# Five operations moved in the hand-written order of a local-attention and expert-adapter kernel

## Chip, cores and metric

The kernel runs on one core of a Trainium2 chip. The metric is the device time of one execution in microseconds, the median of the runs.

## What is computed

Causal attention over 8 batches x 8 heads x 576 tokens x 64 dimensions, in which heads 0 to 3 look back over 32 tokens and heads 4 to 7 over every fourth of 128 tokens; then, on the joined heads as rows of 512, a top-2 mixture of 8 rank-16 adapters that is added to its input. Cut to what matters:

```python
scores = q @ k.T / sqrt(64);  scores = where(mask, scores, -1e9)
x = softmax(scores) @ v                       # (4608, 512) after joining the heads
logits = x @ w_gate                           # (4608, 8)
topk = the two largest logits of a token;  w = softmax of these two
out = x + sum over e in topk of w[e] * ((x @ A[e]) @ B[e])
```

Softmax of two numbers is a sigmoid; the kernel makes it from a tanh of the logit's distance from the mean of the two.

## The kernel before

The work is cut into 8 rows, one for each batch; each row has two halves g = 0, 1 (plain heads, strided heads). `program()` builds named operations, each with an engine and the operations that it depends on. The text `PLAN` (line 605) lists all the names: `ordered()` and `run()` emit the instructions in just that order. An engine works through its own names one after the other, and an instruction whose input isn't there holds up everything behind it on its engine. A number behind @ is the PSUM bank at which a tile begins; a tile waits for all users of the tile that held the bank before it. Waits for other engines are semaphores; a wait that an earlier one already covers is left out.

The operations of a row r that matter here (r = 6 or 7 in the tail):

- `B`, `Bx`: the normalised attention output x is cast to bfloat16 (GpSimd, line 397; ScalarE, line 399). `T`, `U`: TensorE turns it (lines 414, 438). `C`, `Cx`, `Cd`, `Cp`: ScalarE (lines 424, 427, 430, 444, 448) and VectorE (line 431) copy it out of PSUM as xt.
- `Z0`, `Z1`: TensorE multiplies xt by the adapters' A and the gate weights (20 matmuls of 128x136, all TensorE products of this kind go through the helper on line 213). In rows 0 to 6 `Y0`, `Y1` copy the result to SBUF as zs (ScalarE, line 472); in row 7 it is read from PSUM.
- The gate on VectorE: `m0`, `m1` the two largest logits (lines 484, 485), `s12` their sum (line 486), `tt` twice the logit less the sum (line 489), `top` the comparison with the second largest (line 492), `g2` (named g26 for row 6: g2 of row 6) the gate (line 494). Between them stands `th`, the tanh on ScalarE (line 491).
- `gz`: the product of gate and low-rank result (line 499), on GpSimd in rows 0 to 6; in row 7 two pieces `gy`, `gz` on VectorE. `G` (in row 7 `G` and `H`): TensorE turns it (line 504). `gc`, `gn`, `gm`: copies of it out of PSUM, for the two halves (lines 518, 520, 523).
- `D0`, `D1`, `D3`: TensorE multiplies by the adapters' B, four or two matmuls of 128x256; `D2`: four of 64x128 for the last 64 tokens. `A0`, `A1`: VectorE adds the result to x (line 551). `dy`, `A3` and `dx`, `A2`: ScalarE copies a part of the result to SBUF (lines 557, 577), and GpSimd adds it (lines 559, 579).
- `O`: the store of x by SyncE's queue (lines 592, 601). Rows 0 to 4 are stored whole. `O51` waits for A51 and A52, `O50` for A50, A52 and A53, and likewise in row 6; row 7 is stored as `O71` (A71, A72; 576 KB), `O70` (A70; 256 KB) and `O70b` (A72, A73; 320 KB).

D51 is thus row 5's second product, A52 row 5's addition of the last tokens, and so on. The part of the list that makes the tail begins on line 631. What a name waits for is set where it is added, as in

```python
gz = add(f"{a}{r}", "POOL", ("el", 1230), lambda us=us: gates(us, nc.gpsimd), [g2, zc[0], zc[1]] + ([f"G{r - 2}"] if r > 1 else []))
gt.append(add(f"{b}{r}", "PE", ("t", len(us) * nk), lambda us=us, k=k: turn_g(us, k), [gz] + gt, k))
add(f"A{r}2", "POOL", ("el", 512), lambda: [nc.gpsimd.tensor_tensor(ends, ends, two(DY[0]), ALU.add)], [dx] + made)
```

Of the kernel before, what the change touches and what calls it, by code (L numbers as in the profile page):

```python
# [627 lines left out]
Lv701 B60 gz4 E170 E071 s125 G4@0 B61 D31@6 tt5 th5 gn4 V70@1 T60@4  # L628
A31 gc4 V71@5 U6@0 C60 O0 g25 O2 gz5 G5@4 Cp6 Cd6 R70 N70
B70 T61@2 D41@0 D42@3 R71 N71 gn5 A41 C61 dx4 gc5 B71 Bx7 D40@5  # L630
Z06@2 Y06 Z16@4 Y16 A40 m06 A42 D52@3 m16 s126 dx5 top6 U7@7 Cp7
Cd7 tt6 T71@1 Cx7 C71 T70@4 D51@5 A52 th6 g26 A51 D50@0 A50 C70
gz6 Z07@2 Z17 m07 m17 s127 tt7 dy5 G6@5 gc6 O3 O4 O51 D61@0 th7 gn6
D62@7 A53 top7 dx6 g27 D60@5 gy7 gz7 A62 dy6 O50 A61 A63
O61 G7@3 H7 gm7 gn7 gc7 D72@0 dx7 A72 D71@1 A60 D73@6 O60 A71
D70@7 O71 A70 O70 dy7 A73 O70b
"""

# [65 lines left out]
```

## Time and profile before

| what | value |
| --- | --- |
| median of 3 runs | 100.3 us (100.02 to 101.3) |
| the profiled execution's own time | 100.78 us |
| its span, first to last instruction | 99.0 us |
| instructions in the span | 3612 |
| mean granted TensorE clock over the span | 0.976 of full speed |

The span is what the trace covers; the execution's own time holds 1.8 us more around it. Engines are named PE (TensorE's matmuls; PEld are its weight loads), DVE (VectorE), ACT (ScalarE), POOL (GpSimd) and SP (SyncE); a q behind the name is the engine's queue. All times of rows are microseconds from the start of the span. The store O70b is issued at the end of A73, and the span ends once the last store has landed.

### The profile page before, as it was taken

The page shows a single profiled execution, that of the slowest core. Times are in us where ns is not written, and L with a number is a line of the kernel's source. Part 1 is how long each engine was busy: PE and PEld are TensorE (multiplying, and loading weights), DVE is VectorE, ACT ScalarE, POOL GpSimd, SP SyncE. Part 2 cuts the span into 40 slices and gives each one's busy share as a digit, 9 for nine tenths or more (in the row PEclk, how much of TensorE's full clock was granted, in tenths as well). Part 3 has the DMA queues.
Part 4 walks back from the last instruction along what each step waited for, and adds up shares of the span by engine and source line. Part 5 has one row for each costly group of instructions (what it writes and reads, how often), then busy time and mean ns, then how long its engine had stood idle before and what let it go on. Part 6 is the DMA issues. An engine that isn't in the chain of part 4 may idle for free.

```text
span 99.0 us, 3612 instructions
## 1 busy us (share of the span) xinstructions
PE 81.1 (82%) x1587; PEld 59.7 (60%) x1587; DVE 62.4 (63%) x138; ACT 71.4 (72%) x123; POOL 54.6 (55%) x73
## 2 busy tenths in 40 slices
PE   3999969878569989999897979999599988776500
PEld 2443556466446875789666868877487877564300
DVE  5770009506469189459735698779494999979810
ACT  5195692599848974896995689989389989957400
POOL 5999902862449044406941297098076463665820
PEclk9999999999999999999999999999999999999955
DMA  2999999999999999999999999999999996976894
GB/s 18 314 201 211 202 214 224 200 210 226 210 213 213 212 211 214 220 215 207 218 217 213 213 214 213 213 209 186 206 383 425 432 409 287 409 309 251 352 410 194
DMA packets 6095, 24.50 MB, mean 247 GB/s; under 512 B 832, under 2 KB 960, under 8 KB 5440
## 3 DMA queue, kind: packets, MB, share of 16 engines
q0 software_dynamic: 3920, 14.23, 72.1%
q1 hardware_dynamic: 2016, 9.77, 24.6%
q8 instruction: 12, 0.20, 0.8%
q10 hardware_dynamic: 144, 0.28, 0.7%
q14 instruction: 3, 0.02, 0.1%
HBM read 29.07 MB, written 9.44 MB: 389 GB/s over the span
## 4 chain that ended last, share of the span: by engine, by line
PE 45%; DMA 15%; ACT 15%; POOL 10%; DVE 6%; issue 5%; POOLq 0%
PE ps L213 37%; DMA in<-in_qkv_dram 15%; ACT p L351 8%; POOL in L273 7%; PE ps L414 5%; DVE x L390 3%; ACT xt L424 2%; PE ps L504 2%; ACT zs L472 2%; POOL x L559 1%; DVE x L551 1%; POOL xb L397 1%; ACT gn L523 1%; PE ps L438 1%; ACT th L491 1%
## 5 line engine op out<-in xcount | busy, mean ns | idle before, releaser
L397 POOL CAST xb<-x 128x1152 bf16<-128x1152 f32 (+1 forms) x16 | 18.3, 1143 | 25.6 <-DVE x L390 25.6
L351 ACT ACTIVATE p<-ps 128x960 bf16<-128x960 f32 (+1 forms) x32 | 27.6, 900 | 3.4 <-PE ps L213 3.2
L213 PE MATMUL ps<-in,p 128*64 128x130 bf16 (+1 forms) x416 | 21.5, 221 | 4.1 <-ACT p L351 2.9
L390 DVE TENSOR_TENSOR x<-ps,rec 128x1152 f32<-128x1152 f32 x16 | 21.7, 1357 | 0.5
L213 PEld LDWEIGHTS ps<-in,p 128*64 128x64 bf16 (+1 forms) x416 | 17.1, 104 | 7.5 <-ACT p L351 3.9
L551 DVE TENSOR_TENSOR x<-x,ps 128x1024 f32<-128x1024 f32 (+1 forms) x16 | 17.5, 1116 | 3.4 <-PE ps L213 3.4
L387 DVE RECIPROCAL rec<-ps 128x18 f32<-128x18 f32 x16 | 4.3, 270 | 17.7 <-PE ps L213 17.6
L499 POOL TENSOR_TENSOR gz<-zs,g 128x640 bf16<-128x640 f32 x7 | 8.9, 1275 | 9.4 <-DVE g L494 9.4
L213 PE MATMUL ps<-warm 128*128 128x512 f32 x22 | 12.4, 706 | 1.5 <-DVE warm L217 1.5
L213 PEld LDWEIGHTS ps<-in 64*64 64x64 bf16 x576 | 10.9, 106 | 2.7 <-issue 0.7
L213 PE MATMUL ps<-in 64*64 64x96 bf16 (+1 forms) x576 | 11.9, 201 | 0.5 <-issue 0.5
L273 POOL DMA_DIRECT2D in<-in_qkv_dram x22 | 11.8, 581 | 0.8 <-POOLq L687 0.8
L213 PE MATMUL ps<-aw,xt 128*128 128x136 bf16 x160 | 11.4, 223 | 0.4 <-issue 0.3
L424 ACT COPY xt<-ps 128x1024 bf16<-128x1024 bf16 x8 | 8.1, 1011 | 3.4 <-PE ps L414 3.3
L213 PEld LDWEIGHTS ps<-aw,xt 128*128 128x128 bf16 x160 | 9.6, 98 | 1.4 <-issue 0.4
L414 PE MATMUL ps<-one,xb 128*128 128x128 bf16 x128 | 9.6, 219 | 0.9 <-issue 0.8
L414 PEld LDWEIGHTS ps<-one,xb 128*128 128x128 bf16 x128 | 7.6, 98 | 2.2 <-issue 0.9
L427 ACT COPY xt<-ps 128x1024 bf16<-128x1024 bf16 x7 | 7.2, 1034 | 2.3 <-PE ps L414 2.3
L213 PEld LDWEIGHTS ps<-warm 128*128 128x128 f32 x22 | 4.6, 228 | 6.1 <-issue 4.6
L213 PE MATMUL ps<-bt,gn 128*128 128x256 bf16 (+1 forms) x48 | 6.8, 263 | 1.5 <-ACT gn L523 0.8
L213 PE MATMUL ps<-bt,gc 128*128 128x256 bf16 (+1 forms) x48 | 6.6, 255 | 1.5 <-ACT gc L520 1.5
L472 ACT COPY zs<-ps 128x408 f32<-128x408 f32 (+1 forms) x14 | 5.9, 451 | 2.0 <-PE ps L213 1.9
(55 smaller groups left out, 101.6 us busy)
## 6 DMA issues: line engine op xcount, KB each, us to landing
in<-in_qkv_dram POOLq DMA_DIRECT2D x5, 1152.0 KB, 23.2
out_dram<-x SPq DMA_DIRECT2D x5, 1152.0 KB, 7.6
in<-in_qkv_dram POOLq DMA_DIRECT2D x10, 292.5 KB, 24.0
in<-in_qkv_dram POOLq DMA_DIRECT2D x10, 288.0 KB, 8.2
out_dram<-x SPq DMA_DIRECT2D x5, 576.0 KB, 3.0
in<-in_qkv_dram POOLq DMA_DIRECT2D x10, 146.2 KB, 8.1
in<-in_qkv_dram POOLq DMA_DIRECT2D x2, 434.2 KB, 13.8
out_dram<-x SPq DMA_DIRECT2D x1, 320.0 KB, 3.4
```

Of the source, the lines that this page charges most:

```text
L213: return nc.tensor.matmul(o, lhsT=lhsT, rhs=rhs, start=start, stop=stop, skip_group_check=True)
L273: nc.gpsimd.dma_start(out=IN[r % SLOTS][half(a), at : at + n], in_=qkv[r, a, :, at - 2 * VB * a : at - 2 * VB * a + n],)
L351: return [nc.scalar.activation(p[:, :, :].rearrange("p h (s c) -> p h s c", c=PER)[:, :, b0 : b0 + nb, 0:SEG], PS[:, k.at : k.at + 2, 0 : ...
L387: rc = add(f"R{tag}", "DVE", ("el", 60), lambda: [nc.vector.reciprocal(rec[:, :].rearrange("p (b i) -> p b i", b=3), PS[:, k.at : k.at + 3 ...
L390: nm = add(f"N{tag}", "DVE", ("el", XG), lambda: [nc.vector.tensor_tensor(X[r][:, XG * g : XG * g + XG].rearrange("p (b i n) -> p b i n", ...
L397: add(f"B{tag}", "POOL", ("el", cut), lambda: [nc.gpsimd.tensor_copy(XB[r % 2][:, g, 0:cut], X[r][:, XG * g : XG * g + cut])], [nm] + free)
L414: nc.tensor.transpose(tp[j][:, 128 * u : 128 * u + 128], xb[:, g, 256 * u + 128 * j : 256 * u + 128 * j + 128], ident())
L424: return [nc.scalar.copy(xt[:, 0:2, 0:S].rearrange("p j (c i) -> p j c i", c=C)[:, :, :, 0:128], tp.rearrange("p j (i c) -> p j c i", c=C))]
L427: return [nc.scalar.copy(xt[:, 2:4, 0:512], tp)]
L472: zc.append(add(f"Y{st}{r}", "ACT", ("el", len(us) * ZW), lambda us=us, k=k: [nc.scalar.copy(zs[:, us[0] : us[-1] + 1].rearrange("p u n -> ...
L499: return [en.tensor_tensor(GZ[i][:, us[0] : us[0] + n, :].rearrange("p u (e r) -> p u e r", e=E), zv()[:, us[0] : us[0] + n, 0:ER].rearran ...
L551: return [nc.vector.tensor_tensor(v, v, PS[:, k.at : k.at + nk].rearrange("p b n -> p (b n)"), ALU.add)]
```

## The change

Five names move within the list. In row 6 tt6 goes ahead of top6 (VectorE), th6 ahead of C71 (ScalarE), A52 behind gz6 (GpSimd), and G6 ahead of Z07 and Z17 (TensorE). In row 7 D71 goes ahead of D72 (TensorE). The banks stay: G6 still takes bank 5, D71 bank 1, D72 bank 0. SyncE's order of stores is the same.

```diff
-Z06@2 Y06 Z16@4 Y16 A40 m06 A42 D52@3 m16 s126 dx5 top6 U7@7 Cp7
-Cd7 tt6 T71@1 Cx7 C71 T70@4 D51@5 A52 th6 g26 A51 D50@0 A50 C70
-gz6 Z07@2 Z17 m07 m17 s127 tt7 dy5 G6@5 gc6 O3 O4 O51 D61@0 th7 gn6
+Z06@2 Y06 Z16@4 Y16 A40 m06 A42 D52@3 m16 s126 dx5 tt6 top6 U7@7 Cp7
+Cd7 T71@1 Cx7 th6 C71 T70@4 D51@5 g26 A51 D50@0 A50 C70
+gz6 A52 G6@5 Z07@2 Z17 m07 m17 s127 tt7 dy5 gc6 O3 O4 O51 D61@0 th7 gn6
 D62@7 A53 top7 dx6 g27 D60@5 gy7 gz7 A62 dy6 O50 A61 A63
-O61 G7@3 H7 gm7 gn7 gc7 D72@0 dx7 A72 D71@1 A60 D73@6 O60 A71
+O61 G7@3 H7 gm7 gn7 gc7 D71@1 D72@0 dx7 A72 A60 D73@6 O60 A71
```

On TensorE, between row 5's last products and row 6's first (gc1 and gn1 are row 5's, gz0 and gc0 row 6's, xt1 row 7's):

```order
 L213 MATMUL ps<-bt,gn1 128x256 [waits dve_done,act_done]
 L213 MATMUL ps<-bt,gn1 128x256 x3
+L504 MATMUL ps<-one,gz0 128x128 [waits dve_done,pool_done]
+L504 MATMUL ps<-one,gz0 128x128 x4
 L213 MATMUL ps<-aw,xt1 128x136 [waits act_done]
 L213 MATMUL ps<-aw,xt1 128x136 x19
-L504 MATMUL ps<-one,gz0 128x128 [waits dve_done,pool_done]
-L504 MATMUL ps<-one,gz0 128x128 x4
 L213 MATMUL ps<-bt,gc0 128x256 [waits dve_done,act_done]
 L213 MATMUL ps<-bt,gc0 128x256 x3
```

G6's five transposes, with their waits for VectorE and GpSimd, now stand ahead of Z07 and Z17; D61, the next below, keeps its place behind both.

On VectorE, row 6's gate part (zs0, tt0, th0 and g20 are row 6's) up to A51 and A50:

```order
 L485 MAX mx0<-zs0 128x8
 L486 TENSOR_REDUCE s120<-mx0 128x5 [waits dve_done]
+L489 SCALAR_TENSOR_TENSOR tt0<-zs0,s120 128x40 [waits dve_done]
 L492 TENSOR_TENSOR top0<-zs0,mx0 128x40
-L489 SCALAR_TENSOR_TENSOR tt0<-zs0,s120 128x40 [waits dve_done]
 L431 COPY xt1<-ps 128x512 [waits pe_done]
-L494 SCALAR_TENSOR_TENSOR g20<-th0,top0 128x40 [waits act_done]
+L494 SCALAR_TENSOR_TENSOR g20<-th0,top0 128x40 [waits dve_done,act_done]
 L551 TENSOR_TENSOR x5<-x5,ps 128x1024 [waits pe_done]
 L551 TENSOR_TENSOR x5<-x5,ps 128x512 [waits pe_done]
```

The difference tt6 and the comparison change places; Cx7 (line 431) still stands ahead of the gate g26.

On GpSimd, the casts and additions around row 6's gate product:

```order
 L397 CAST xb1<-x7 128x512 [waits dve_done]
 L579 TENSOR_TENSOR x4<-x4,awf 128x2x128 [waits act_done]
-L579 TENSOR_TENSOR x5<-x5,awf 128x2x128 [waits act_done]
 L499 TENSOR_TENSOR gz0<-zs0,g20 128x640 [waits dve_done]
+L579 TENSOR_TENSOR x5<-x5,awf 128x2x128
 L559 TENSOR_TENSOR x5<-x5,in0 128x512 [waits act_done]
 L579 TENSOR_TENSOR x6<-x6,awf 128x2x128 [waits act_done]
```

Row 5's addition A52 (x5) now follows the product gz6 and stands just ahead of A53.

## Rows read from the trace of the kernel before

**Rows 1.** The page's busy time of each engine (us, share of the span, instructions), and two of its lines of 40 slices of 2.47 us each: the granted TensorE clock in tenths of full speed, and the mean busy share of the 16 DMA engines in tenths.

```profile
PE 81.1 (82%) x1587; PEld 59.7 (60%) x1587; DVE 62.4 (63%) x138; ACT 71.4 (72%) x123; POOL 54.6 (55%) x73
...
PEclk9999999999999999999999999999999999999955
DMA  2999999999999999999999999999999996976894
```

**Rows 2.** The chain of work that ended last, from 84 us on; columns: start us, us, engine, tile and line.

```profile
84.43 0.67 DVE top L492
...
86.43 1.36 PE ps L213 x20
87.79 0.29 PE ps L504 x5
...
93.44 1.27 POOL x L559
```

**Rows 3.** Two windows of the tail; columns: stretch, its length in us, then busy us and instructions of PE, PEld, DVE, ACT and POOL, then granted clock, DMA share and GB/s.

```profile
90.50:92.00 1.50, 0.69 (x12) 0.44 (x10) 1.50 (x3) 1.11 (x3) 1.50 (x2) 1.00 0.12 46
92.00:97.70 5.70, 0.96 (x8) 0.61 (x8) 1.95 (x3) 0.96 (x2) 2.27 (x3) 0.70 1.02 414
```

**Rows 4.** Stores: the issue of O61 on SyncE's queue (start us, us), then what the list of DMA issues tells of O61 alone and of O70b alone (KB, us from issue to landing).

```profile
91.19 0.33 SPq L601 DMA_DIRECT2D out_dram<-x  x1
...
out_dram<-x SPq DMA_DIRECT2D x1, 576.0 KB, 2.8
...
out_dram<-x SPq DMA_DIRECT2D x1, 320.0 KB, 3.4
```

**Rows 5.** VectorE in order of time, row 6's gate part and the two operations behind it; columns: start us, us, engine, line, operation, tiles, shape, count.

```profile
84.26 0.17 DVE L486 TENSOR_REDUCE s<-mx 128x5 f32<-128x10 f32 x1
84.34 0.75 DVE L492 TENSOR_TENSOR top<-zs,mx 128x40 f32<-128x40 f32 x1
85.02 0.19 DVE L489 SCALAR_TENSOR_TENSOR tt<-zs,s 128x40 f32<-128x40 f32 x1
85.13 0.41 DVE L431 COPY xt<-ps 128x512 bf16<-128x512 bf16 x1
85.51 0.20 DVE L494 SCALAR_TENSOR_TENSOR g<-th,top 128x40 f32<-128x40 f32 x1
85.63 1.21 DVE L551 TENSOR_TENSOR x<-x,ps 128x1024 f32<-128x1024 f32 x1
```

**Rows 6.** GpSimd in order of time in the same stretch, with the idle time ahead and what ended it in brackets.

```profile
84.31 0.73 POOL L579 TENSOR_TENSOR x<-x,awf 128x256 f32<-128x256 f32 x1 [1.64 <-ACT awf L577]
85.79 1.28 POOL L499 TENSOR_TENSOR gz<-zs,g 128x640 bf16<-128x640 f32 x1 [0.75 <-DVE g L494]
```

**Rows 7.** A GpSimd cast around 58.4 us, VectorE's comparison (line 492) of another row beside it, and the durations of all seven comparisons of that form (ns, least/median/most).

```profile
58.41 1.18 POOL L397 CAST xb<-x 128x1152 bf16<-128x1152 f32 x1
...
58.76 0.90 DVE L492 TENSOR_TENSOR top<-zs,mx 128x40 f32<-128x40 f32 x1
...
L492 DVE TENSOR_TENSOR top<-zs,mx x7: 190/200/992, 25.8 to 84.3; 128x40 f32<-128x40 f32 x7
```

**Rows 8.** ScalarE in order of time; first the piece around row 6's tanh, then row 7's tanh and the copy behind it.

```profile
84.47 0.59 ACT L430 COPY xt<-ps 128x512 bf16<-128x512 bf16 x1
85.24 0.24 ACT L491 ACTIVATE th<-tt 128x40 f32<-128x40 f32 x1 [0.18 <-DVE tt L489]
85.38 0.99 ACT L424 COPY xt<-ps 128x1024 bf16<-128x1024 bf16 x1
...
88.64 0.24 ACT L491 ACTIVATE th<-tt 128x40 f32<-128x40 f32 x1
88.78 0.63 ACT L523 COPY gn<-ps 128x576 bf16<-128x576 bf16 x1
```

**Rows 9.** The seven gate products on GpSimd (ns, least/median/most).

```profile
L499 POOL TENSOR_TENSOR gz<-zs,g x7: 1271/1274/1281, 26.7 to 85.8; 128x640 bf16<-128x640 f32 x7
```

**Rows 10.** TensorE's matmuls in order of time; D51, D50, Z07 with Z17, and G6, one row each; then one row that holds D72's last two and D71's four.

```profile
84.72 0.60 PE L213 MATMUL ps<-bt,gc 128*128 128x256 bf16 x4
85.69 0.60 PE L213 MATMUL ps<-bt,gn 128*128 128x256 bf16 x4 [0.37 <-DVE xt L431]
86.43 1.36 PE L213 MATMUL ps<-aw,xt 128*128 128x136 bf16 x20
87.63 0.44 PE L504 MATMUL ps<-one,gz 128*128 128x128 bf16 x5
...
91.74 0.79 PE L213 MATMUL ps<-bt,gc 128*64 128x128 bf16 x6
```

**Rows 11.** VectorE in order of time, row 7's gate part: m17, tt7, g27, and A61 further down.

```profile
87.83 0.32 DVE L485 MAX8 mx<-ps 128x8 f32<-128x8 f32 x3 [0.23 <-PE ps L213]
...
88.38 0.20 DVE L489 SCALAR_TENSOR_TENSOR tt<-ps,s 128x40 f32<-128x40 f32 x1
...
88.92 0.20 DVE L494 SCALAR_TENSOR_TENSOR g<-th,top 128x40 f32<-128x40 f32 x1 [0.23 <-ACT th L491]
...
89.95 1.21 DVE L551 TENSOR_TENSOR x<-x,ps 128x1024 f32<-128x1024 f32 x1
```

**Rows 12.** Two windows behind the last matmul, columns as in group 3.

```profile
92.96:94.30 1.34, 0.00 (x1) 0.00 (x0) 1.34 (x2) 0.41 (x1) 1.10 (x2) 1.00 1.00 413
94.30:99.00 4.70, 0.00 (x0) 0.00 (x0) 0.08 (x1) 0.00 (x0) 0.41 (x1) 0.50 0.74 297
```

## Prediction

> **What bounds the kernel now.** I read the page first [rows 1]: no engine is busy over 82% of the span, the granted clock is full until the last two slices, and the DMA engines are at nine tenths or more in nearly all slices, with a notch just ahead of the end. Then the chain of waits [rows 2]: at 84.43 us it runs through row 6's comparison, at 86.43 through row 7's twenty router products, behind them row 6's five transposes, and it ends in A73 on GpSimd. The reader is to see that Z07 and Z17 stand ahead of G6 on this chain, and that the comparison takes 0.67 us of it for 40 elements a partition.
>
> Then the windows of the DMA engines [rows 3]: from 90.50 to 92.00 they are 0.12 busy, and from 92.00 to 97.70 they are full (share 1.02, 414 GB/s). The bytes are those of the last five stores: 3 x 576 + 256 + 320 = 2304 KB, 2.36 MB, and at 414 GB/s that is 5.7 us, the whole window. So from O61 on the stores run back to back, and the end is fixed by the moment at which O61 is issued, 91.19 us [rows 4], so long as the later ones are issued in time. O61 took 2.8 us on idle engines, 1.42 of it transfer and so 1.4 fixed; O70b's 320 KB would take 1.4 + 0.8 = 2.2 by itself and took 3.4 [rows 4]. It stood 1.2 us in line. That is the cover of everything that only A72, A73, O71 and O70b wait for.
>
> O61 waits for A61, which ends at 89.95 + 1.21 = 91.16 [rows 11]. On VectorE A61 stands behind row 7's whole gate part (m17, tt7, top7, g27, gy7, gz7). So what sets the end is: C70, Z07, Z17, m17, tt7, th7, g27, the gate products, A61, O61, the stores.
>
> **The change, part by part.** No instruction is added or removed; their places on four engines change. All times up to 84.43 stay, since nothing ahead is touched.
>
> A52 behind gz6. Row 6's comparison took 0.75 us while A52 ran beside it: 84.34 to 85.09, against 84.31 to 85.04 for A52 [rows 5, 6]. The same form takes 0.19 to 0.20 elsewhere; 0.90 beside a cast at 58.41, ending (59.66) 0.07 after it [rows 7]. I take it that the comparison waited for GpSimd to finish. With A52 gone GpSimd is idle until gz6, so 0.55 goes.
>
> tt6 ahead. It needs the sum that ends at 84.43 [rows 5]. With the hand-off of 0.03 (tt6's end at 85.21 to th6 at 85.24 [rows 5, 8]) and 0.20 of duration [rows 11] it runs 84.46 to 84.66; before it ended at 85.21. The comparison starts 0.08 before that end, as its neighbours overlap [rows 5], and runs 84.58 to 84.77.
>
> th6 ahead of C71. 84.69 to 84.93, on a ScalarE that was free for C71 at 84.47 [rows 8]. C71 is issued 0.14 later (85.24 to 85.38 [rows 8]), so 84.83 to 85.42, 0.36 later than before; C70 follows with an overlap of 0.10 and runs 85.32 to 86.31, 0.06 sooner than before. Z07 follows C70's end by 0.06 [rows 8, 10]: its inputs are there at 86.37, against 86.43. That is all the front of the chain can win, however soon the tanh is.
>
> g26 and gz6. Cx7 still stands ahead of g26 and takes 0.41 [rows 5]: 84.69 to 85.10. g26 goes 85.07 to 85.27, gz6 0.08 behind [rows 5, 6], 85.35; all seven products on GpSimd took 1.27 to 1.28 [rows 9], so it ends at 86.63, 0.44 sooner than before. A51 needs D51, which ends at 85.32 [rows 10], and with 1.21 [rows 5] is done at 86.56, just ahead of it.
>
> G6 ahead of Z07. TensorE works in order. G6 waits for gz6 and for A51, which empties its bank: 86.63 + 0.06 = 86.69. Behind it stand Z07, Z17, D61 and all the rest. The five transposes hold the issue for 0.29 [rows 2], so Z07 starts at 86.98 instead of 86.43: **0.55 late**. TensorE sits idle from D50's end (86.05 by C71's end of 85.42) to 86.69, with Z07 ready from 86.37.
>
> What G6 wins is hidden. It ends at 87.14 rather than 88.07 [rows 10], so ScalarE copies gc6 0.93 sooner and D61 can follow Z17 at 88.18. But A61 stands on VectorE behind row 7's gate products, and gn6 on ScalarE stands behind th7; both wait for Z17. th7 started at 88.64, 0.06 behind tt7's end (88.38 + 0.20 [rows 11]), held until gc6 was through; at the usual 0.03 that is a slack of 0.03 and no more. With Z17 0.55 later m17 starts at 88.38, tt7 ends at 89.13, th7 starts at 89.16: **0.52 late**. g27, the products and A61 follow at the same distances as before: A61 ends at 91.68 and O61 is issued at 91.71, 0.52 late. gn6 starts at 89.30, and D62, D60 and G7 behind it move likewise.
>
> A52 and A53 later. A52 now takes 86.59 to 87.32 (0.73 [rows 6]), and O51 and O50, which wait for it, are issued up to 0.5 later. Both land in front of the notch of 90.50 to 92.00, which is 1.5 us wide [rows 3] and moves to about 92.5. They cost nothing; if the notch were gone they would cost 0.5.
>
> D71 ahead of D72. D71 needs only gc7 and goes first; D72 falls behind its four matmuls, by at most 0.60 (the duration of the same four of D51 [rows 10]; D72's last two and D71 together took 0.79 [rows 10]). So dx7, A72 and A73 are at most 0.52 + 0.60 = 1.12 late, while the stores in front are 0.52 late; the line of 1.2 that O70b stood in covers the 0.60. Cost 0; without that line it would be up to 0.60. That A71 is up to 0.35 nearer wins nothing, O71 being in the line too.
>
> **Sum.** -0.06 (copies) + 0.61 (Z07 kept back beyond its inputs) - 0.03 (slack at th7) = +0.52 us. The profiled execution took 100.78 us: 99.0 of span and 1.8 around it; with 0.52 it would be 101.30. It lies 0.5 above the median of the runs, 100.3, so the forecast is 100.3 + 0.5 = **100.8 us**. Bounds of the one unknown, when G6's wait ends: Z07 can't start before its inputs, which gives -0.1; if the comparison's stall stays, gz6 ends 0.56 later, at 87.19, and the sum is +1.1.
>
> **Rivals.** (1) *No loss.* GpSimd's spans are rough; if G6 is let go well before 86.63, the wait on TensorE shrinks. For it: nothing in the rows, only that bookkeeping. Against: the products' narrow spread [rows 9], and g26's 0.08 to gz6. At best -0.1: 100.2 us.
>
> (2) *The stall stays.* If the comparison waited for something else than GpSimd, top6 still takes 0.75 behind tt6, Cx7 and g26 follow at 85.25 and 85.63, gz6 ends at 87.19, Z07 starts at 87.53: 1.1 late, 101.4 us. Against it stand both ends that follow GpSimd's by 0.05 to 0.07 [rows 5 to 7].
>
> (3) *The clock falls in the new gap; slower than before.* TensorE has nothing between D61's end (88.18 + 0.60 = 88.79) and D62 (gn6's end, 89.30 + 0.63 = 89.93 [rows 8], and a hand-off): some 1.2 us. After the last matmul the clock stayed at full for 1.34 us and then fell to 0.50 [rows 12], that is to 1.2 GHz. From 89.98 on the columns of D62, D60, G7 with H7 and D71 would take twice their time: at most 0.3 + 0.6 + 0.6 + 0.6 = 2.1 more ahead of A71, by rows of like shape [rows 2, 10]. Of this the line of the stores takes 0.6 to 1.2. That leaves 0.9 to 1.5, say 1.4 on top of 0.52: 102.2 us. It decides if the fall comes before G7. Against: TensorE worked densely for some us ahead of that gap, and in 90.50 to 92.00, with TensorE less than half busy, it was full [rows 3].
> The Trainium skill ("TensorE: Matmul & The Clock Gate", Part 1, What's actually happening) says that the throttled state is the default and that recent activity lifts it, which speaks against a change that opens gaps. By that rule alone the sum would be this rival's; the trace agrees that a pause in which nothing is issued ends in the lower level, and shows no matmul that ran there.
>
> (4) *A port wait in another place.* A52 and A53 now end about 0.25 later than before. Row 7's g27 reads two SBUF tiles as the comparison did; at 89.44 it lies some 0.9 behind A53. If GpSimd slipped by that much, g27 would wait up to 1.3: 102.1 us.
> The Trainium skill ("SBUF — State Buffer", SBUF: two separate sides) calls the pair of ports that VectorE and GpSimd share an exclusive lock, held for the whole instruction. Row 6's comparison agrees; by the rule row 7's comparison, which reads PSUM, is free of it, and no run here shows more.
>
> **Chances.** Forecast (+0.4 to +0.7) 0.62; no loss 0.2; stall stays 0.07; clock 0.08; port wait 0.03. The runs of before spread from 100.02 to 101.3, so a median of a few is good to about 0.4: the range goes from no loss less 0.4 to the stall's 101.4 and a little more, 99.8 to 101.7. About 2% is what a measurement of this kernel tells from no change, 98.3 to 102.3: same 0.92; slower 0.06, half of the clock and port rivals and a little; faster 0.02, since no case reaches it.
>
> **What would show it.** Row 6's comparison at 0.2 us and tt6's end near 84.7; gz6 near 85.35; on TensorE G6 ahead of Z07 with a new wait for GpSimd ahead of it, Z07 near 87.0; gc6 near 87.2 but th7 near 89.2; O61 near 91.7; the DMA engines full from there to the end. It is wrong if Z07 starts before 86.6, if A61 ends before 91.2, or if the stores no longer run back to back behind O61, for then the end hangs on A73.

## The result

| | before | changed |
| --- | --- | --- |
| median of 22 runs each | 100.52 us | 101.1 us |
| least | 99.95 us | 100.68 us |
| profiled execution, span | 99.0 us | 99.7 us |

The ratio is 1.0055 with a 95% interval of 1.0028 to 1.0082: slower by 0.55 us (0.3 to 0.8), where 0.52 was forecast. By the 2% measure it is no change; by the interval it is a small loss. Medians here and below are of all runs, while ratios and intervals leave out runs that took over 1.5% longer than the fastest of the same kernel.

The profiled execution of the changed kernel was 0.21 us late before the change begins: row 6's sum ends at 84.48 + 0.17 = 84.65 instead of 84.43. So from here on times are counted from the end of that sum, written s+. It is the same instruction in all kernels. From execution to execution its end moved, by up to 0.8 us against that of the kernel before and by 2.1 in e2, while the distance to O61's issue stayed: s+6.76 in the kernel before, and again in e3 and e11 below, whose front is the same.

VectorE after, in order of time (start us, us, engine, line, operation, tiles, shape, count): row 6's sum, tt6, the comparison, Cx7 and g26; row 7's m17 and tt7; A61.

```profile
84.48 0.17 DVE L486 TENSOR_REDUCE s<-mx 128x5 f32<-128x10 f32 x1
84.68 0.20 DVE L489 SCALAR_TENSOR_TENSOR tt<-zs,s 128x40 f32<-128x40 f32 x1
84.79 0.20 DVE L492 TENSOR_TENSOR top<-zs,mx 128x40 f32<-128x40 f32 x1
84.91 0.42 DVE L431 COPY xt<-ps 128x512 bf16<-128x512 bf16 x1
85.24 0.19 DVE L494 SCALAR_TENSOR_TENSOR g<-th,top 128x40 f32<-128x40 f32 x1
...
88.54 0.32 DVE L485 MAX8 mx<-ps 128x8 f32<-128x8 f32 x3 [0.46 <-PE ps L213]
89.09 0.20 DVE L489 SCALAR_TENSOR_TENSOR tt<-ps,s 128x40 f32<-128x40 f32 x1
...
90.64 1.21 DVE L551 TENSOR_TENSOR x<-x,ps 128x1024 f32<-128x1024 f32 x1
```

The comparison takes 0.20 instead of 0.75 [rows 5], and tt6 runs ahead of it at once. GpSimd and ScalarE after:

```profile
85.51 1.28 POOL L499 TENSOR_TENSOR gz<-zs,g 128x640 bf16<-128x640 f32 x1 [2.38 <-DVE g L494]
86.75 0.73 POOL L579 TENSOR_TENSOR x<-x,awf 128x256 f32<-128x256 f32 x1
```

```profile
84.91 0.24 ACT L491 ACTIVATE th<-tt 128x40 f32<-128x40 f32 x1
85.05 0.57 ACT L430 COPY xt<-ps 128x512 bf16<-128x512 bf16 x1
85.52 1.02 ACT L424 COPY xt<-ps 128x1024 bf16<-128x1024 bf16 x1
...
89.33 0.24 ACT L491 ACTIVATE th<-tt 128x40 f32<-128x40 f32 x1 [1.33 <-DVE tt L489]
```

gz6 starts at s+0.86 (s+1.36 before [rows 6]) with GpSimd idle for 2.38 us ahead of it, and A52 follows. The tanh starts at s+0.26 and C71 0.14 behind it. C70 starts at s+0.87, where it was at s+0.95 [rows 8]: the earlier tanh bought 0.08 there. Row 7's tanh waited 1.33 us for tt7 on an idle ScalarE, where before it followed gc6 without a gap. TensorE after: D50, G6, Z07 with Z17, and D62's first two.

```profile
85.67 0.61 PE L213 MATMUL ps<-bt,gn 128*128 128x256 bf16 x4 [0.20 <-ACT xt L430]
86.88 0.44 PE L504 MATMUL ps<-one,gz 128*128 128x128 bf16 x5 [0.59 <-POOL gz L499]
87.15 1.35 PE L213 MATMUL ps<-aw,xt 128*128 128x136 bf16 x20
...
90.14 0.25 PE L213 MATMUL ps<-bt,gn 128*64 128x128 bf16 x2 [1.20 <-ACT gn L523]
```

This is the loss. TensorE stands 0.59 us waiting for GpSimd ahead of G6, and Z07 starts at s+2.50 instead of s+2.00 [rows 10]. G6 itself is 0.97 earlier, at s+2.23 against s+3.20, and it wins nothing: D62 waits 1.20 for gn6, which ScalarE makes behind row 7's tanh. The chain of waits after (start us, us, engine, tile and line) now runs through gz6 into G6, where it ran through Z07 and Z17 into G6 [rows 2]:

```profile
85.51 1.29 POOL gz L499
86.80 0.08 issue
86.88 0.44 PE ps L504 x5
87.32 1.20 PE ps L213 x20
...
90.72 1.13 DVE x L551
```

A61 ends at s+7.20 instead of s+6.73. The stores after: O61's issue, its time to landing and O70b's; then three windows (columns as in [rows 3]).

```profile
91.88 0.33 SPq L601 DMA_DIRECT2D out_dram<-x  x1
...
out_dram<-x SPq DMA_DIRECT2D x1, 576.0 KB, 2.8
...
out_dram<-x SPq DMA_DIRECT2D x1, 320.0 KB, 3.2
```

```profile
88.94:90.14 1.20, 0.00 (x0) 0.00 (x1) 0.94 (x5) 0.76 (x2) 0.00 (x0) 1.00 1.02 419
91.25:92.50 1.25, 0.52 (x8) 0.33 (x6) 1.25 (x3) 1.03 (x3) 1.25 (x2) 1.00 0.00 0
92.50:98.40 5.90, 1.16 (x12) 0.55 (x9) 2.13 (x3) 0.88 (x2) 2.40 (x3) 0.73 0.98 400
```

O61 is issued at s+7.23 instead of s+6.76, 0.47 late, lands 2.8 us after its issue as before [rows 4], and from 92.50 to 98.40 the DMA engines are full. The notch ahead of it is empty. From O61's issue to O70b's landing it is 6.95 us (91.88 to 98.83), and it was 6.97 before (91.19 to 98.16): the whole line moved with its first store.

### The profile page after: what moved, and what is told of

Read it like the earlier page. It is cut to its first block, busy times and chain, and to the rows that moved or that the text cites. A ratio compares the mean times of both kernels' runs of the same rounds, so it can differ in the third digit from the quotient of the medians.

```text
span 99.7 us, 3613 instructions
## 1 busy us (share of the span) xinstructions
PE 81.4 (82%) x1587; PEld 59.7 (60%) x1587; DVE 62.0 (62%) x138; ACT 71.0 (71%) x123; POOL 54.4 (55%) x73
## 4 chain that ended last, share of the span: by engine, by line
PE 57%; ACT 16%; DVE 13%; issue 5%; POOL 4%
PE ps L213 49%; ACT p L351 10%; PE ps L414 5%; DVE x L551 5%; DVE x L390 3%; PE ps L504 2%; POOL gz L499 1%; POOL x L559 1%; ACT in L263 1%; POOL xb L397 1%; ACT zs L472 1%; ACT xt L424 1%; PE ps L438 1%; ACT xt L427 1%; DVE gz L499 1%
## 5 line engine op out<-in xcount | busy, mean ns | idle before, releaser
L213 PE MATMUL ps<-warm 128*128 128x512 f32 x22 | 12.9, 729 | 1.5 <-DVE warm L217 1.5
(55 smaller groups left out, 101.1 us busy)
```

The source lines that it names most:

```text
L213: return nc.tensor.matmul(o, lhsT=lhsT, rhs=rhs, start=start, stop=stop, skip_group_check=True)
```

## The experiments

Medians below stand beside runs of the kernel before on the same chip, 23 to 31 of them in each group. Most intervals are near 0.4% on either side, so the distances in the traces carry what the ratios can't.

**G6 put back (e1).** The changed kernel with

```diff
-gz6 A52 G6@5 Z07@2 Z17 m07 m17 s127 tt7 dy5 gc6
+gz6 A52 Z07@2 Z17 m07 m17 s127 tt7 dy5 G6@5 gc6
```

> The changed kernel with G6 put back behind Z17; the other four moves stay. Theory (the loss is G6 on TensorE ahead of Z07): the loss is gone, 0.06 us below before, a ratio to before of about 0.999, Z07 starting 0.06 behind C70's end and no TensorE wait for GpSimd ahead of it. Rival (A52's and the stores' delay, or D71 ahead of D72, bears the loss): the ratio stays near 1.005.

Measured: 100.62 us against 100.59, ratio 0.9983 (0.9943 to 1.0023). TensorE, Z07 with Z17 and then G6 (one of its five transposes is missing from the records):

```profile
86.61 1.36 PE L213 MATMUL ps<-aw,xt 128*128 128x136 bf16 x20 [0.30 <-ACT xt L424]
87.80 0.39 PE L504 MATMUL ps<-one,gz 128*128 128x128 bf16 x4
```

The sum ended at 84.66, so Z07 is at s+1.95, and O61 was issued at 91.36, s+6.70: 0.05 and 0.06 sooner than before. The wait left is for C70. With all other moves in place the loss is gone, so it is G6's place that makes it.

**G6 alone ahead (e2).** The kernel before with

```diff
-gz6 Z07@2 Z17 m07 m17 s127 tt7 dy5 G6@5 gc6
+gz6 G6@5 Z07@2 Z17 m07 m17 s127 tt7 dy5 gc6
```

> The kernel before with G6 alone put ahead of Z07; A52, tt6, th6 and D71 stay as before. Theory: G6 waits for gz6 as late as it was before, 0.44 us later than in the changed kernel, so Z07 starts 1.0 us later than before and the end is 0.95 later: ratio 1.0095, twice the loss of the change. Rival (the other moves cause the loss): between 1.000 and 1.003.

Measured: 101.92 us against 100.59, ratio 1.0115 (1.0063 to 1.0167). The span of its trace is left aside, since TensorE's clock was at its lower level for a while in the middle of that execution. From 57.6 to 95.0 us, though, the granted clock was 1.00, and that stretch holds G6's wait and O61's issue:

```profile
89.25 0.45 PE L504 MATMUL ps<-one,gz 128*128 128x128 bf16 x5 [0.84 <-POOL gz L499]
...
94.26 0.33 SPq L601 DMA_DIRECT2D out_dram<-x  x1
```

The sum ended at 86.56, so O61 is issued at s+7.70, 0.94 later than before (0.95 expected), behind a wait of 0.84 where the changed kernel's was 0.59. The loss is twice that of the change, as the later gz6 has it: the other moves softened G6's wait and did not cause it.

**G6 between (e4).** The changed kernel with

```diff
-gz6 A52 G6@5 Z07@2 Z17 m07
+gz6 A52 Z07@2 G6@5 Z17 m07
```

> The changed kernel with G6 between Z07 and Z17. Theory: gz6 is done when Z07 has been issued, so G6 waits for nothing; Z17 and what follows it are late by G6's 0.29 us of issue less 0.06 and 0.03, 0.2 us: ratio 1.002. Rival (G6 is dear wherever it stands ahead of Z17, or the loss lies elsewhere): 1.005.

Measured: 101.03 us against 100.59, ratio 1.0031 (0.9988 to 1.0074). TensorE: Z07, G6, Z17, and further down D71.

```profile
85.61 0.65 PE L213 MATMUL ps<-aw,xt 128*128 128x136 bf16 x8 [0.30 <-ACT xt L424]
86.10 0.44 PE L504 MATMUL ps<-one,gz 128*128 128x128 bf16 x5
86.38 0.87 PE L213 MATMUL ps<-aw,xt 128*128 128x136 bf16 x12
...
91.02 0.92 PE L213 MATMUL ps<-bt,gc 128*128 128x256 bf16 x4 [0.73 <-DVE gc L518]
```

G6 now follows Z07 without a wait, and Z17 follows G6 at once. The sum ended at 83.67; O61 was issued at 90.62, s+6.95, 0.19 later than before, as expected. The ratio alone, whose interval holds 1.000 and 1.005, would settle nothing. In this execution there is a second thing: D71 took 0.92 where the changed kernel's took 0.61. Two windows around it (columns as in [rows 3]):

```profile
90.60:91.02 0.42, 0.00 (x0) 0.00 (x1) 0.42 (x2) 0.42 (x2) 0.42 (x1) 1.00 0.00 0
91.02:93.00 1.98, 1.98 (x12) 0.99 (x12) 1.55 (x2) 0.51 (x3) 0.87 (x2) 0.54 0.81 335
```

The granted clock fell within D71, behind a pause of 0.73 us without a matmul, and O71 was issued 0.24 us too late for its turn in the line (at 93.62; O60 landed at 94.76, and here a store of 576 KB in line lands 1.38 after the one ahead of it, and no sooner than 2.76 after its own issue). This is the mechanism of the prediction's third rival, later in the tail than it was put there and with a small price.

**D71 alone (e3).** The kernel before with `gc7 D71@1 D72@0 dx7 A72 A60` for `gc7 D72@0 dx7 A72 D71@1 A60`.

> The kernel before with D71 alone put ahead of D72. Theory (A73 is covered by the line of stores): dx7 and A73 end 0.3 to 0.6 us later against O61's issue, O70b lands at the same distance from O61's issue, 7.0 us: ratio 1.000 within 0.002. Rival (the end hangs on A73, as the chain of waits has it): 0.3 to 0.6 us more, ratio 1.003 to 1.006.

Measured: 100.96 us against 100.59, ratio 1.002 (0.9982 to 1.0057), which decides nothing by itself. In the trace A72 ends 0.47 later against O61's issue than before (92.86 - 90.38 = 2.48, against 2.01 from [rows 4] and the end of A72 at 93.20), A73 starts 0.19 later against it, and O70b lands 6.95 us after O61's issue, against 6.97. In that execution the swap cost nothing.

**A73 held back (e5, e6).** The kernel before with additions into a spare tile on GpSimd between A72 and A73: one of 256 columns (e5), two of 512 (e6).

```diff
-D70@7 O71 A70 O70 dy7 A73 O70b
+D70@7 O71 A70 O70 dy7 J0 J1 A73 O70b
```

> The kernel before with one addition on GpSimd into a spare tile (128x256, 0.73 us like A72) between A72 and A73; the outputs are the same. Theory (O70b stands 1.2 us in line): the time stays, ratio 1.000 within 0.002. Rival (the end hangs on A73): 0.7 us more, 1.007.

> The kernel before with two additions on GpSimd into a spare tile (128x512, 1.27 us each) between A72 and A73: A73 ends 2.3 us later. Theory: the line covers 1.1 to 1.2 of it and 1.1 shows, ratio 1.011. Rival (the end hangs on A73): 1.023.

Measured: e5 100.4 us against 100.42, ratio 0.9992 (0.9952 to 1.0031); e6 100.93, ratio 1.0046 (1.0014 to 1.0079). GpSimd in e6: A72, the two additions, A73.

```profile
91.75 0.73 POOL L580 TENSOR_TENSOR x<-x,awf 128x256 f32<-128x256 f32 x1 [0.20 <-ACT awf L578]
92.56 2.15 POOL L591 TENSOR_TENSOR scr<-x 128x512 f32<-128x512 f32 x2
94.67 1.26 POOL L560 TENSOR_TENSOR x<-x,btf 128x512 f32<-128x512 f32 x1
```

The additions took 2.15 us rather than 2.5 and filled a wait that A73 had anyway, so A73 starts at s+10.97, 1.96 later than before (93.44 - 84.43 = 9.01); in e5 it is 0.41 later. Of the 1.96, 0.46 (0.14 to 0.79) shows. Expected were 1.1, and 2.3 by the rival: by the difference the cover is 1.2 to 1.8 us, and my 1.1 had A73 too late. O70b's landing in e6 (KB, us from its issue):

```profile
out_dram<-x SPq DMA_DIRECT2D x1, 320.0 KB, 2.1
```

2.1 us instead of 3.4 [rows 4]: issued this late it no longer stands in line.

**O61 held back (e7).** The kernel before with O61 made to wait for A60 too, and its name put behind D73, just ahead of O60; no other name moves. Of the edit, the wait:

```diff
+                if (r, g) == (B - 2, 1):
+                    parts = ((0, XG, [f"A{r}1", f"A{r}2", f"A{r}0"]),)
```

> The kernel before with the store O61 alone made to wait for A60 as well; no other engine's order or waits change. O61 is issued at A60's end, 0.97 us later than before. Theory (the stores run back to back from O61 on): the end is 0.95 us later, ratio 1.0095. Rival (the end hangs on A73 or O71): no change, 1.000 to 1.002.

Measured: 101.5 us against 100.42, ratio 1.0092 (1.0056 to 1.0128). O61's issue, its landing and O70b's:

```profile
91.91 0.33 SPq L603 DMA_DIRECT2D out_dram<-x  x1
...
out_dram<-x SPq DMA_DIRECT2D x1, 576.0 KB, 2.8
...
out_dram<-x SPq DMA_DIRECT2D x1, 320.0 KB, 3.8
```

The sum ended at 84.19, so O61 is at s+7.72, 0.96 late, and the time is 0.92% up. No engine's work moved. So the end hangs on O61's issue, though the chain of waits names A73. O70b now stands in line longer, 3.8 us to its landing instead of 3.4 [rows 4].

**O51 held back (e11).** The same kind of edit for O51, which waits for A53 too and stands behind it in the list: in the profiled executions O51 is issued 1.5 us later, at s+3.94 instead of s+2.44.

> The kernel before with the store O51 alone made to wait for A53, so that it is issued about 1.4 us later; the other engines' order and waits are the same. Forecast's claim (O51 and O50 land in the notch of 90.5 to 92.0): ratio 1.000 within 0.002. Rival (one lagging DMA engine is still at O50 when O61 begins, so a late O51 pushes the whole line): 0.4 to 1.4 us more, ratio 1.004 to 1.014.

Measured: 100.47 us against 100.47, ratio 0.9996 (0.9966 to 1.0027). The late A52 and O51 of the change are free, as forecast, but not because they land in front of the notch. In the kernel before, O51 lands at 90.98, 1.40 us behind the store O4 (89.57), and O50 at 92.33, which is 1.1 behind O61's issue. In e11 O51 is issued 1.5 later and still lands 1.38 behind O4 (91.08 against 89.70). So O51 stands in line behind O4, and its own issue has time to spare. O50 landed 1.84 behind O61's issue in this execution and O61 took 3.2 us instead of 2.8, as the rival has it; but as O51 landed no further behind O4 than elsewhere, its late issue did not cause that.

**tt6 alone (e10).** The kernel before with tt6 ahead of top6 and A52 where it was.

> The kernel before with tt6 alone put ahead of top6; A52 still runs on GpSimd at that moment. If what stalled the comparison is GpSimd's instruction and any operation with two SBUF inputs meets it, tt6 is now the one that takes about 0.7 us and ends with A52, top6 takes 0.2, and th6 starts no earlier. If only the comparison's kind of instruction is stalled, tt6 takes 0.2, th6 starts 0.5 earlier and top6 keeps its 0.75. The whole time can't tell them apart.

One run, 100.29 us, which says nothing of the time. VectorE (the sum, tt6, the comparison) and GpSimd (A52) in it:

```profile
83.90 0.17 DVE L486 TENSOR_REDUCE s<-mx 128x5 f32<-128x10 f32 x1
84.10 0.64 DVE L489 SCALAR_TENSOR_TENSOR tt<-zs,s 128x40 f32<-128x40 f32 x1
84.66 0.18 DVE L492 TENSOR_TENSOR top<-zs,mx 128x40 f32<-128x40 f32 x1
```

```profile
83.95 0.73 POOL L579 TENSOR_TENSOR x<-x,awf 128x256 f32<-128x256 f32 x1 [1.40 <-ACT awf L577]
```

The stall has moved to whichever of the two comes first: tt6 takes 0.64 and ends at 84.74, 0.06 behind A52's end. It belongs to GpSimd's instruction and not to the comparison. The tanh starts at s+0.70, 0.11 sooner than before and not 0.5.

**A better version, tried (e8, e9).** e1 showed that Z07 waits for C70. e8 is e1 with the tanh back behind C71:

```diff
-Cd7 T71@1 Cx7 th6 C71 T70@4 D51@5 g26
+Cd7 T71@1 Cx7 C71 T70@4 D51@5 th6 g26
```

> The changed kernel with G6 back behind Z17 and th6 back behind C71; A52 behind gz6, tt6 ahead of top6 and D71 ahead of D72 stay. Theory: C71 isn't pushed back by the tanh and ScalarE doesn't wait for tt6, so C70 starts at 85.1 instead of 85.38 and Z07 0.28 us earlier than before; gz6 is still in time: 0.25 us below before, ratio 0.9975, better than both. Rival (C70 isn't what Z07 waits for, or O71's issue holds the end): 0.999 to 1.000.

Measured: 100.98 us against 100.42, ratio 1.0013 (0.9976 to 1.005): not the gain expected. ScalarE's C71, tanh and C70; then the stores: the landings of O4 and O50, O61's issue, O61's landing.

```profile
84.45 0.59 ACT L430 COPY xt<-ps 128x512 bf16<-128x512 bf16 x1
84.93 0.24 ACT L491 ACTIVATE th<-tt 128x40 f32<-128x40 f32 x1
85.07 1.01 ACT L424 COPY xt<-ps 128x1024 bf16<-128x1024 bf16 x1
```

```profile
out_dram<-x SPq DMA_DIRECT2D x1, 1152.0 KB, 6.4
...
out_dram<-x SPq DMA_DIRECT2D x1, 576.0 KB, 4.1
...
90.89 0.33 SPq L601 DMA_DIRECT2D out_dram<-x  x1
...
out_dram<-x SPq DMA_DIRECT2D x1, 576.0 KB, 3.3
```

The front did what it should. The sum ended at 84.41, C70 starts at s+0.66 (s+0.95 before), Z07 0.28 earlier and O61 at s+6.48, 0.28 earlier. But O61 took 3.3 us to land instead of 2.8, since O50 was still on its way: it landed at 92.84, and O61 1.40 behind it. The distance from O61's issue to O70b's landing is 7.49 instead of 6.97. O50 needs 2.8 to 4.6 us to land in these traces, and where it lands more than 1.4 after O61's issue, O61 is late by the excess (in e1, e6, e8 and e11). In those executions an earlier O61 is given back. O50 itself stands in line: in these traces it lands 1.33 to 1.46 behind O51, and O51 1.37 to 1.41 behind O4 (1.63 in the changed kernel's, which had O4 early and O51 late), while O4's 1152 KB took 4.5 to 6.5 us from issue to landing. In the four executions where O61 was late, O4 took 6.3 us or more. Whether that accounts for the whole of the missing 0.25 us in the runs is not shown.

e9 keeps A52 ahead of gz6 but lets it run earlier (D52 ahead of Z16, dx5 ahead of Y06), so that O51 is not late:

> The run before this one (G6 and th6 back, D71 ahead of D72, tt6 ahead of top6), with D52 between Z06 and Z17's row-6 partner Z16 and dx5 ahead of Y06, so that A52 runs on GpSimd from about 83.4 to 84.1, ahead of row 6's gate part and ahead of gz6. Theory: the comparison takes 0.2 us without A52 having to move behind gz6, O51 is issued when A51 ends (no later than in the kernel before, counted from Z07), Z07 starts 0.28 us earlier against the sum of row 6 or as early on the whole; ratio 0.997 to 0.998. Rival (one lagging DMA engine fills the notch in part of the executions, so an earlier O61 buys nothing): O61 is issued 0.2 to 0.3 earlier and lands no earlier, ratio 1.000.

Measured: 100.3 us against 100.47, ratio 0.9985 (0.9964 to 1.0007). The comparison took 0.19 and O51 was issued at 86.74, but D52 ahead of Z16 made row 6's sum 0.5 us later against O4's issue, and O61 0.14 later against it, than in e3 and e11, whose front is that of the kernel before. It is no better than before beyond what can be measured, and no version here is shown to beat it.

## Why the prediction was right

- *The stall goes with A52.* Right: 0.75 to 0.20, tt6's end from s+0.78 to s+0.23 (forecast s+0.23). e10 shows the cause.
- *The earlier tanh wins 0.06 at C70.* Right: 0.08 in the trace, 0.05 at Z07 in e1. It stands ahead of C71 and pushes it back; e8 shows that behind C71 0.28 was to be had at Z07.
- *gz6 0.44 sooner.* Right: 0.50.
- *G6 holds Z07 back by 0.55.* Right: 0.50 in the trace, gone in e1, doubled in e2, down to 0.19 at O61 in e4. That is the term that makes the sum. In the sum's own terms: the copies gave 0.05 (0.06 forecast), Z07 was kept back beyond its inputs by 0.55 (0.61; s+2.50 against s+1.95 in e1), the slack at th7 took 0.03 off, and O61 was 0.47 late (0.52).
- *G6's gain is hidden behind the tanh of row 7 and the gate products.* Right: gn6 was 0.47 later although G6 was 0.97 earlier.
- *The end is O61's issue and 5.7 us of stores.* Right: e7 moved that store alone and the time followed, 0.92% for 0.96 us.
- *O51 and O50 late at no cost.* The cost was right, by e11. The reason was not: they do not both land in front of the notch, since in the trace of before O50 lands 1.1 us behind O61's issue. What covers them is the 1.4 us by which O50 may land behind that issue before O61 is late, and the line behind O4 in which they mostly stand anyway. So O61's 2.8 us in the kernel before were not on idle engines either; it took the same 2.8 in the changed kernel, where O50 had landed (91.71) before O61's issue (91.88).
- *D71 at no cost under the line.* Held in the trace; the ratio of e3 leaves up to 0.5% open. The cover was put at 1.2 us; e6 puts it at 1.2 to 1.8.
- *The rivals.* The first falls, since TensorE did wait for GpSimd's end; the second with the comparison's 0.20. The port wait did not occur: g27 took 0.20. The clock stayed full through the new pause of 1.20 us in the profiled execution (window 88.94 to 90.14), but e4's execution shows that it can fall in the tail, ahead of the last matmuls.

The forecast of 100.8 us stood on the first median, 100.3 from three runs. Beside the 100.52 of 22 runs the same 0.52 makes 101.04, and 101.1 was measured, so the difference of 0.3 is mostly that of the starting point.

What was off was outside the sum: the reason why O51 and O50 are free, e6's expected loss, with A73 put too late, and e8's expected gain, with the line of stores taken to begin at O61's issue alone, where O50's landing can hold it too.

## What to carry to other kernels

Before an operation is hoisted on an engine that works in order, compare when its input arrives with when the operation it passes could start: the difference is paid by everything behind, and the early result is worth only what its first consumer, on its own engine, can use. Where the last stores run back to back, the end is set by the issue of the first of them, or by the store that this one still stands behind, and the chain of waits, which ends in the last instruction, points to the wrong place; delay one store alone to see it. A gap in an engine's timeline isn't the only sign of a wait: an operation of 40 elements that takes 0.75 us instead of 0.2 was waiting too.

## What the runs showed of the hardware

- A VectorE operation with both inputs in SBUF that starts beside a GpSimd addition or cast ends 0.05 to 0.07 us behind it, whichever operation it is: top6 before (0.75 us), tt6 in e10 (0.64), the comparison of [rows 7] (0.90), against 0.18 to 0.20 with GpSimd idle. The wait is shown as duration. Row 7's comparison, with one input in PSUM and one in SBUF, is free of it: in e8 it started at 88.20 in the middle of A53 (87.41 to 88.67) and took 0.19. The Trainium skill ("SBUF — State Buffer", SBUF: two separate sides) says that the shared pair of ports is an exclusive lock, which whichever starts first gets for its whole instruction while the other blocks; these rows agree.
- The clock fell to its lower level in e4 at 91.17 us, two microseconds ahead of the last matmul, behind pauses of 1.01 and 0.73 us; in the changed kernel's execution it stayed full through 1.20 and 0.73 until behind the last matmul.
- O61's 576 KB took 2.8 us to landing wherever O50 was out of its way; O51 and O50, of the same size, took 2.7 to 4.7, since they land one behind the other behind O4. Why O4's 1152 KB took 4.5 us in one execution and 6.5 in another wasn't found.
